# Low halves of the first weights and of V's weights on VectorE alone, and the last result's operands scaled ahead of their products

## The chip, the cores and the metric

The kernel runs on one core of one Trainium2 chip. The metric is the time of one execution on the device, in microseconds (us); smaller is better. The engines are named as in the profile: PE is TensorE's matmul, PEld its weight load, DVE is VectorE, ACT is ScalarE, POOL is GpSimd and SP is SyncE, whose queue issues most of the transfers.

## The reference, cut to what matters

For an input x of 2048 rows by 512 columns, attention with a sliding window of 256 (32 heads of 16) and a gated feed-forward layer are computed from the same x, and a gate per row mixes them:

```
x = A_x
g = sigmoid((x * gate_w).sum(-1, keepdims=True))
a = attention(x @ wqkv, window 256) @ wo
b = (silu(x @ w_gate) * (x @ w_up)) @ w_down
out = g * a + (1 - g) * b
```

## The kernel before

**Products.** Every fp32 operand of a product is split into a high half, rounded to the matmul's own fp32 format, and a low half, which is the rest. A product of two operands is three matmuls: high by high, high by low, low by high. The function `split` (L67 to L73) makes the halves: the high one is a copy (L70, here always on ACT), and the low one is the subtraction of L73, `lo = src - hi`, on the engine that the caller names. The instruction at L73 waits for the one at L70.

**Order.** The order of the instructions on each engine is the order in which the program text emits them (a manual schedule); each engine goes through its own list in that order and waits where an operand is not there. A tile name has a fixed number of buffers; a tile that takes over a buffer waits for the last use of the one before.

**Start.** SP's queue loads, in this order, pieces of the first two groups' query and key weights (`wqk`), the four parts of x's first 512 rows (`xT[0]`), the four parts of V's weights (`wv`) and the rest of x. `split_wq(g, n, lo_eng)` splits piece n of the weights of group g: piece 0 is the first 128 columns, piece 1 the other 384. `split_x(c, ks)` splits parts ks of x's chunk c. PE begins with `proj` of groups 0 and 1 on x's chunk 0 (24 matmuls into the tile `pa`, three for a group and part in turn), then `vproj(0)` to `vproj(3)`, V for four blocks of 128 rows (12 matmuls each into the tile `pb`, which has two buffers; `put_v` on ACT empties them, L443), then `proj` on chunks 1 to 3 (L232 for all of these). `fill_rows` sets memory on POOL, and POOL also makes the low halves of the projections' results (`split_qk`).

**Middle.** Attention's scores, weights and values for eight groups are woven with the feed-forward's first two products; PE has no gap there.

**End.** The feed-forward's last product is computed as a seven-product block scheme; `ITEMS` lists its steps in order, and `halve(e)` splits the operand of a step four steps ahead into `HALF[e]` (tiles `hh`, `hl`). The last stage of the scheme is stage 4, and the last three of its steps (from `end`) are drained by hand: the first of the two results, (2, 2), gets its three products with `block(e, (0,))`; then the last result, (2, 3), gets its three products in two halves of 256 columns, with an own PSUM tile `pa`. `GATE[1]` holds 1 - g, and `scaled` multiplies a result by it (L952), adds the part from attention (L954) and sends it (L956). For (2, 3) `rest` is that sum without the last three steps. The end before the change is:

```
scaled(2, 3, rest, two[1], send=False)
for e in ITEMS[end:]:
    block(e, (0,))
scaled(2, 2, t, two[0])
...
    nc.vector.tensor_tensor(out=part[:, cols], in0=ps, in1=GATE[1][:, 2, cols], op=ALU.mult)
    nc.vector.tensor_tensor(out=part[:, cols], in0=part[:, cols], in1=rest[:, cols], op=ALU.add)
    nc.sync.dma_start(place(2, 3)[:, cols], part[:, cols])
```

Of the kernel before, what the change touches and what calls it, by code (L numbers as in the profile page):

```python
# [9 lines left out]
F32 = mybir.dt.float32  # L10
F32R = mybir.dt.float32r
AF = mybir.ActivationFunctionType
ALU = mybir.AluOpType
# [3 lines left out]
P = 128  # L17
S, D, H, DH, W, F = 2048, 512, 32, 16, 256, 1792
NK = D // P
NB = S // P  # L20
CH = 512
# [15 lines left out]
def gated_mix(ctx, tc, xT, xn, wqk, wv, wo, wgu, wd, gw, outT):  # L37
# [4 lines left out]
    nc = tc.nc  # L42
# [18 lines left out]
    ring = ctx.enter_context(tc.tile_pool(name="ring", bufs=2))  # L61
# [6 lines left out]
    def split(hi, lo, src, hi_eng, lo_eng):  # L68
        if hi_eng is nc.scalar:
            nc.scalar.copy(hi, src)  # L70
        else:
            hi_eng.tensor_copy(hi, src)
        lo_eng.tensor_tensor(out=lo, in0=src, in1=hi.bitcast(F32), op=ALU.subtract)  # L73

    def fetch(src, raw=None):

        raw = ring.tile([P, D], F32, name="raw", bufs=1) if raw is None else raw
        nc.sync.dma_start(raw, src)
        return raw

    def by_k(t):
        return t.rearrange("p (k n) -> p k n", k=NK)
# [11 lines left out]
    def run(gen, n=None):  # L94

        while n is None or n > 0:
            if next(gen, run) is run:
                break
            n = n and n - 1
# [73 lines left out]
    def prefetch():  # L173
        if WKEYS:
            PEND.append(weights(WKEYS[0], lo_eng=nc.vector if WKEYS.pop(0) == ('f', NF - 1, 0) else nc.gpsimd))
# [25 lines left out]
    with ExitStack() as A:  # L201
# [14 lines left out]
        def kept():  # L216
            return sm.tile([P, CH], F32, name="ev", bufs=EV)
# [10 lines left out]
        def whole(pool, name, todo, done):  # L228

            ps = pool.tile([P, CH], F32, name=name)  # L230
            for n, (w, x) in enumerate(todo):
                nc.tensor.matmul(ps, w, x, start=n == 0, stop=n == len(todo) - 1)  # L232
                if n < len(todo) - 1:
                    yield
            done(ps)
            yield
# [166 lines left out]
        wvh = vpool.tile([P, NK, D], F32R, name="wvh")  # L403
        wvl = vpool.tile([P, NK, D], F32R, name="wvl")
# [8 lines left out]
        def split_wq(g, n, lo_eng):  # L413
            if n == 0:
                WT["p", g] = [ring.tile([P, D], F32R, name=w) for w in ("wh", "wl")]
            hi, lo = (w[:, QUARTERS[n]] for w in WT["p", g])
            split(hi, lo, WQ[g][:, QUARTERS[n]], nc.scalar, lo_eng)
            if n == 1:
                WT["p", g] = [by_k(w) for w in WT["p", g]]
# [3 lines left out]
        def fill_rows(tiles, value, hf, eng):  # L423
            for t in tiles:
                eng.memset(halves_of(t)[hf].bitcast(F32), value)
# [3 lines left out]
        def fill_v(t):  # L429
            nc.gpsimd.memset(t, 0.0)  # L430
            for i in range(2):
                nc.gpsimd.memset(t[:, :, i, :68].rearrange("p g (j e) -> p g j e", e=17)[:, :, :, DH], 1.0)
# [3 lines left out]
        def v_products(b):  # L436
            c, o = divmod(b * P, CH)
            return [(xt[c][:, k, o:o + P], wt[:, k]) for k in range(NK)
                    for xt, wt in ((xhi, wvh), (xhi, wvl), (xlo, wvh))]

        def put_v(b, ps):
            t = vs[b // 2 % 2]
            nc.scalar.copy(t[:, :, b % 2, :68].rearrange("p g (j e) -> p g j e", e=17)[:, :, :, :DH],  # L443
                           ps.rearrange("p (g j e) -> p g j e", j=4, e=DH))
            if b % 2:
                nc.gpsimd.dma_start(vd[:, :, b - 1:b + 1].rearrange("g p b e -> p g (b e)"),
                                    t.rearrange("p g b e -> p g (b e)"))

        def vproj(b):
            return whole(pp, "pb", v_products(b), lambda ps: put_v(b, ps))  # L450
# [11 lines left out]
        def split_x(c, ks=range(NK)):  # L462
            for k in ks:
                split(xhi[c][:, k], xlo[c][:, k], xraw[2 * c + k // 2][k % 2], nc.scalar, nc.vector)

        for c in range(NCH):
# [7 lines left out]
            if c == 0:  # L474
                wvraw = [fetch(wv[:, k], kept()) for k in range(NK)]
        split_wq(0, 0, nc.gpsimd)
        split_x(0, range(1))
        split_wq(1, 0, nc.vector)
        split_wq(0, 1, nc.gpsimd)
        fill_rows(KT[0], 1.0, 0, nc.gpsimd)  # L480
        split_x(0, range(1, 2))
        split_wq(1, 1, nc.vector)
        split_x(0, range(2, NK))
        for k in range(NK):
            split(wvh[:, k], wvl[:, k], wvraw[k], nc.scalar, nc.vector if k % 2 else nc.gpsimd)
        prefetch()
        both = [proj(g, 0, pp, "pa") for g in range(2)]
        for k in range(NK):
            for gen in both:
                run(gen, 3)  # L490
        split_x(1)
        fill_v(vs[1])
        fill_rows(QT[0], 0.0, 1, nc.gpsimd)
        fill_rows(KT[0], 1.0, 1, nc.gpsimd)
        for b in range(2):
            run(vproj(b))
        split_x(2)
        for b in range(2, 4):
            run(vproj(b))
# [198 lines left out]
        for t in range(G * NB + 1):  # L698
            g, i = divmod(t, NB)
            d, part = divmod(t, NSLOT)  # L700
# [31 lines left out]
    with ExitStack() as B:  # L732
        got = B.enter_context(tc.tile_pool(name="got", bufs=10, side="right"))
        hp = B.enter_context(tc.tile_pool(name="hp", bufs=LEAD + 2, side="right"))
# [5 lines left out]
        def column():  # L740
            return hp.tile([P, CH], F32, name="sg", bufs=4)

        def taken(src):
            t = got.tile([P, CH], F32, name="got")
            nc.sync.dma_start(t, src)
            return t

        def load_wo(k):
            raw = taken(wo[:, k])
            return lambda: split(woh[:, k], wol[:, k], raw, nc.scalar, nc.vector)  # L750
# [35 lines left out]
        ITEMS = [("a", c, k) for c in range(NCH) for k in range(NK)]  # L786
# [4 lines left out]
        SRC, HALF, PARTS = {}, {}, {}  # L791
# [34 lines left out]
        def spare(m):  # L826
            return PLACE[5][:, 2 + m] if m < 2 else PLACE[6][:, m]
# [65 lines left out]
        GATE = {}  # L893
# [71 lines left out]
        def after(p, pr):  # L965

            two = bank(p, pr)
            for d in range(2):
                m = 2 * pr + d
                if p == 1:  # L970
                    JOBS.append(lambda d=d, m=m: nc.scalar.copy(saved(m), two[d]))
                if p == 5:
                    JOBS.append(lambda d=d, m=m: nc.scalar.copy(saved(4 + m), two[d]))
                if p == 6:
                    JOBS.append(lambda d=d, m=m: nc.vector.tensor_tensor(out=spare(m), in0=two[d], in1=saved(4 + m), op=ALU.subtract))
                if p == 2:
                    JOBS.append(lambda d=d, m=m: combined(2 * pr, d, two[d], saved(m), ALU.add))
                if p == 7:
                    JOBS.append(lambda d=d, m=m: combined(2 * pr + 1, 2 + d, two[d], saved(4 + m), ALU.subtract))
                if p == 3:  # L980
                    JOBS.append(lambda d=d, m=m: combined(2 * pr + 1, d, two[d], spare(m), ALU.add))
                if p == 4 and pr == 0:
                    JOBS.append(lambda d=d: scaled(2 * pr, 2 + d, column(), two[d]))

        late = [load_wo(k) for k in range(NK)]
        for e in ITEMS[:LEAD]:
            load(e)
# [21 lines left out]
        end = len(ITEMS) - 3  # L1009

        DO = {}

        def on(n, f, *args):
            DO.setdefault(n, []).append(lambda: f(*args))

        for j in range(2 * NP):
            two = divmod(j, 2)
            n = WO + j
# [20 lines left out]
        for i in range(NP):  # L1039
            n = WO + 57 + 4 * (i // 2) + i % 2 - (i == 6)  # L1040
            steps(n, (n + 6, n + 7), negated, NP + i)
        for n, e in enumerate(ITEMS[:end]):
            if n + LEAD + AHEAD < WO:
                load(ITEMS[n + LEAD + AHEAD])
            for f in DO.pop(n, ()):
                f()
            while rows and at[(*rows[0], 0)] <= n + 6:
                load_sum(*rows.pop(0))
            if n + LEAD < len(ITEMS):
                halve(ITEMS[n + LEAD])  # L1050
            if JOBS:
                JOBS.pop(0)()
            if e[0] == "a":
                multiply_a(*e[1:])
                continue
            p, k, pr = e
            block(e)
            HALF.pop(e)
            if k == NP - 1:
                after(p, pr)  # L1060
        while JOBS:
            JOBS.pop(0)()
        two, t, part, rest = bank(4, 1), *(column() for _ in range(3))
# [4 lines left out]
        for cols in (slice(0, CH // 2), slice(CH // 2, CH)):  # L1068
            ps = pp.tile([P, CH], F32, name="pa")[:, cols]
            for n, (p, k, pr) in enumerate(ITEMS[end:]):  # L1070
                hh, hl = HALF[p, k, pr]
                mm3(ps, [(block_weights(p, k, 1), (hh[:, cols], hl[:, cols]))], start=n == 0, stop=n == 2)
            nc.vector.tensor_tensor(out=part[:, cols], in0=ps, in1=GATE[1][:, 2, cols], op=ALU.mult)
            nc.vector.tensor_tensor(out=part[:, cols], in0=part[:, cols], in1=rest[:, cols], op=ALU.add)
            nc.sync.dma_start(place(2, 3)[:, cols], part[:, cols])


# [32 lines left out]
```

## Time and profile before

| | before |
|---|---|
| median of 3 runs | 803.44 us (803.0 to 803.46) |
| the profiled execution's own time | 803.47 us |
| its span, first to last instruction | 801.8 us |
| PE busy | 795.2 us, 99% of the span |
| DVE busy | 627.3 us, 78% |
| ACT busy | 432.4 us, 54% |
| POOL busy | 346.2 us, 43% |
| granted TensorE clock | 1.0 of full speed |

The span is what the rows below show; 1.67 us of the profiled execution's time lie around it. A row of the timeline has the start, the duration, the engine, the line, the operation, the tiles written and read, the shapes and the count, and in brackets how long the engine stood idle before it and what ended that.

### The profile page before, as it was taken

To read this page: it belongs to the slowest core of one execution; us is meant where nothing else is said; L and a number is where in the kernel's file an instruction comes from. 1 tells how busy PE (TensorE), PEld (TensorE's weight loads), DVE (VectorE), ACT (ScalarE), POOL (GpSimd) and SP (SyncE) were. 2 spreads that over 40 slices of the span, in tenths; PEclk is the share of its full clock that TensorE was granted. 3 is DMA by queue.
4 is the path that set the end of the run, shared out by engine and by line. 5 is a ranking of instruction groups with operands and counts; after the bars stand their busy time and mean duration, and the time that the engine had idled before them with its cause. 6 is when DMAs were issued, how large, how long until landed. Compare 5 with 4: busy or idle time off the path is not lost.

```text
span 801.8 us, 21443 instructions
## 1 busy us (share of the span) xinstructions
PE 795.2 (99%) x8247; PEld 697.1 (87%) x8247; DVE 627.3 (78%) x1686; ACT 432.4 (54%) x883; POOL 346.2 (43%) x647
## 2 busy tenths in 40 slices
PE   8999999999999999999999999999999999999998
PEld 7888999989889989889998988888988888888886
DVE  6397687878887787878777878888675478899896
ACT  6412656666566566555666656555643235554642
POOL 7821546564546556544656454546740111000212
PEclk9999999999999999999999999999999999999999
DMA  8675414434252453351444516435627898718435
GB/s 298 171 200 164 141 57 135 119 114 137 71 164 78 117 167 94 113 163 54 134 119 130 152 46 200 134 99 181 195 100 240 283 342 300 290 56 275 93 54 104
DMA packets 62107, 121.88 MB, mean 152 GB/s; under 512 B 10868, under 2 KB 19828, under 8 KB 61748
## 3 DMA queue, kind: packets, MB, share of 16 engines
q1 hardware_dynamic: 54900, 99.27, 40.1%
q0 software_dynamic: 7104, 21.24, 9.0%
q8 instruction: 65, 1.06, 0.6%
q14 instruction: 38, 0.31, 0.1%
HBM read 55.97 MB, written 39.34 MB: 119 GB/s over the span
## 4 chain that ended last, share of the span: by engine, by line
PE 96%; DVE 2%; DMA 1%; SPq 0%; POOL 0%; issue 0%; ACT 0%
PE pa L252 24%; PE pb L252 24%; PE ps L302 7%; PE ps L344 5%; PE ps L368 5%; PE ps L89 4%; PE ps L90 4%; PE ps L88 4%; PE pb L368 4%; PE pb L232 2%; PE pb L89 2%; PE pa L89 2%; PE pa L90 2%; PE pb L90 2%; PE pa L88 2%; PE pb L88 2%
## 5 line engine op out<-in xcount | busy, mean ns | idle before, releaser
L304 DVE CUSTOM_DVE_ANT_0 ps<-ps,mask 128x384 f32<-128x384 f32 (+2 forms) x512 | 268.4, 540 | 99.4 <-PE ps L344 52.3
L346 ACT ACTIVATE pt<-ps 128x384 f32<-128x384 f32 (+2 forms) x512 | 238.0, 474 | 127.8 <-PE ps L344 68.0
L348 POOL TENSOR_SCALAR_AFFINE_SELECT pt<-pt 128x256 f32<-128x256 f32 x256 | 110.2, 431 | 198.6 <-ACT pt L346 196.8
L344 PE MATMUL ps<-q,k 64*128 64x384 f32 (+2 forms) x512 | 162.3, 334 | 0.0
L302 PE MATMUL ps<-k,q 63*128 63x384 f32 (+2 forms) x512 | 159.8, 332 | 0.5 <-DVE mx L304 0.5
L252 PE MATMUL pb<-xhi,wh 64*128 64x512 f32 x512 | 116.9, 395 | 0.0
L252 PE MATMUL pb<-xlo,wh 64*128 64x512 f32 x512 | 115.6, 391 | 0.0
L252 PE MATMUL pb<-xhi,wl 64*128 64x512 f32 x512 | 115.6, 391 | 0.0
L252 PE MATMUL pa<-xhi,wh 64*128 64x512 f32 x512 | 115.3, 393 | 0.0
L252 PE MATMUL pa<-xlo,wh 64*128 64x512 f32 x512 | 114.2, 391 | 0.0
L252 PE MATMUL pa<-xhi,wl 64*128 64x512 f32 x512 | 114.2, 391 | 0.0
L302 PEld LDWEIGHTS ps<-k,q 63*128 63x128 f32 x512 | 88.7, 185 | 14.1 <-DVE mx L304 3.7
L351 POOL TENSOR_SCALAR_AFFINE_SELECT pt<-pt 128x256 f32<-128x256 f32 x224 | 98.6, 440 | 0.0
L344 PEld LDWEIGHTS ps<-q,k 64*128 64x128 f32 x512 | 91.1, 184 | 4.9 <-ACT pt L346 0.2
L304 DVE DVE_READ_ACCUMULATOR2_ANT mx<- 128x1 f32 x512 | 71.3, 139 | 0.0
L368 PE MATMUL ps<-pt,vg 64*32 64x320 f32 (+4 forms) x1408 | 70.6, 344 | 0.0
L368 PE MATMUL pb<-pt,vg 64*32 64x256 f32 (+3 forms) x1360 | 69.9, 349 | 0.0
L252 PEld LDWEIGHTS pb<-xhi,wh 64*128 64x128 f32 x512 | 62.8, 185 | 4.1 <-DVE o L385 0.3
L252 PEld LDWEIGHTS pb<-xhi,wl 64*128 64x128 f32 x512 | 62.4, 184 | 3.5
L252 PEld LDWEIGHTS pa<-xhi,wl 64*128 64x128 f32 x512 | 61.1, 185 | 3.9
L252 PEld LDWEIGHTS pb<-xlo,wh 64*128 64x128 f32 x512 | 62.5, 185 | 0.2
L252 PEld LDWEIGHTS pa<-xhi,wh 64*128 64x128 f32 x512 | 60.5, 186 | 1.8
(305 smaller groups left out, 1604.5 us busy)
## 6 DMA issues: line engine op xcount, KB each, us to landing
kept_h<-ev SPq DMA_DIRECT2D x52, 256.0 KB
od<-o POOLq DMA_DIRECT2D x32, 256.0 KB, 3.7
raw<-wgu SPq DMA_DIRECT2D x28, 256.0 KB
q<-xhi SPq DMA_DIRECT2D x56, 128.0 KB
k<-xhi SPq DMA_DIRECT2D x56, 128.0 KB
outT<-sg POOLq DMA_DIRECT2D x28, 256.0 KB, 4.4
vd<-vs POOLq DMA_DIRECT2D x8, 672.0 KB, 4.8
vg<-vd SPq DMA_DIRECT2D x32, 168.0 KB
```

The lines of the kernel that those rows point to most:

```text
L88: nc.tensor.matmul(ps, lh, rh, start=start and i == 0, stop=False, skip_group_check=skip)
L89: nc.tensor.matmul(ps, lh, rl, start=False, stop=False, skip_group_check=skip)
L90: nc.tensor.matmul(ps, ll, rh, start=False, stop=stop and i == n - 1, skip_group_check=skip)
L232: nc.tensor.matmul(ps, w, x, start=n == 0, stop=n == len(todo) - 1)
L252: mm = nc.tensor.matmul(ps[me], w[r], x[r], start=not second and i == 0, stop=bool(second) and i == n - 1)
L302: nc.tensor.matmul(ps[:, :n], QT[g % 2][pr][r, q0:q0 + P], KT[g % 2][pr][r, k0:k0 + n], start=True, stop=True)
L304: mx = nc.vector.tensor_tensor_reduce(out=ps[:, :n], in0=ps[:, :n], in1=mask[:, 3 * P - n:], scale=1.0, scalar=NEG, op0=ALU.add, op1=ALU.m ...
L344: nc.tensor.matmul(ps[:, :n], KT[g % 2][pr][r, k0:k0 + P], QT[g % 2][pr][r, k0:k0 + n], start=True, stop=True)
L346: BEHIND.append(nc.scalar.activation(pt[:, j, :n], ps[:, :n], AF.Exp, scale=SCALE))
L348: nc.gpsimd.affine_select(out=pt[:, :, :P], in_=pt[:, :, :P], pattern=[[0, 2], [1, P]], compare_op=ALU.is_ge, fill=0.0, base=0, channel_mu ...
L351: nc.gpsimd.affine_select(out=pt[:, :, 2 * P:], in_=pt[:, :, 2 * P:], pattern=[[0, 2], [-1, P]], compare_op=ALU.is_ge, fill=0.0, base=-1, ...
L368: nc.tensor.matmul(AV[g, c][h][32 * j:32 * j + 32, q0 - c * CH:q1 - c * CH], VG[4 * g + kb // 4][o, kb % 4, 17 * j:17 * j + 32], PT[g, kb, ...
```

## The change

At the start, the low half of piece 1 of group 0's weights goes from POOL to DVE, and so do the low halves of parts 0 and 2 of V's weights (parts 1 and 3 were on DVE). The split of x's chunk 1 is moved from before `vproj(0)` to two parts behind `vproj(0)` and two behind `vproj(1)`; `fill_v` and the two `fill_rows` of POOL that stood behind it now stand ahead of the products. At the end, a new function `scaled_halves` multiplies the operand of each of the last three steps by the gate, into the single buffer of the tile `raw`, and splits the product; it is called three times in a row when the loop over the steps is over, ahead of `rest`. The last result's products then take these halves, and the multiplication by the gate behind the products is gone.

```diff
         split_wq(1, 0, nc.vector)
-        split_wq(0, 1, nc.gpsimd)
+        split_wq(0, 1, nc.vector)
...
-            split(wvh[:, k], wvl[:, k], wvraw[k], nc.scalar, nc.vector if k % 2 else nc.gpsimd)
+            split(wvh[:, k], wvl[:, k], wvraw[k], nc.scalar, nc.vector)
...
-        split_x(1)
         fill_v(vs[1])
         fill_rows(QT[0], 0.0, 1, nc.gpsimd)
         fill_rows(KT[0], 1.0, 1, nc.gpsimd)
         for b in range(2):
             run(vproj(b))
+            split_x(1, range(2 * b, 2 * b + 2))
...
+        SCALED = []
+
+        def scaled_halves(i):
+
+            e = ITEMS[end + i]
+            raw = ring.tile([P, D], F32, name="raw", bufs=1)
+            nc.vector.tensor_tensor(out=raw, in0=PARTS["v", e[1], e[2]], in1=GATE[1][:, 2], op=ALU.mult)
+            SCALED.append([ring.tile([P, D], F32R, name=w) for w in ("wh", "wl")] if i < 2 else
+                          [hp.tile([P, CH], F32R, name=w) for w in ("hh", "hl")])
+            split(*SCALED[i], raw, nc.scalar, nc.vector)
...
         DO = {}
+        DO[end] = [lambda i=i: scaled_halves(i) for i in range(3)]
...
+        for f in DO.pop(end):
+            f()
         while JOBS:
             JOBS.pop(0)()
...
-                hh, hl = HALF[p, k, pr]
+                hh, hl = SCALED[n]
                 mm3(ps, [(block_weights(p, k, 1), (hh[:, cols], hl[:, cols]))], start=n == 0, stop=n == 2)
-            nc.vector.tensor_tensor(out=part[:, cols], in0=ps, in1=GATE[1][:, 2, cols], op=ALU.mult)
-            nc.vector.tensor_tensor(out=part[:, cols], in0=part[:, cols], in1=rest[:, cols], op=ALU.add)
+            nc.vector.tensor_tensor(out=part[:, cols], in0=ps, in1=rest[:, cols], op=ALU.add)
             nc.sync.dma_start(place(2, 3)[:, cols], part[:, cols])
```

## Rows read from the trace of the kernel before

**Rows 1.** The page: PE's busy time, and the chain that ended last.

```profile
PE 795.2 (99%) x8247; PEld 697.1 (87%) x8247; DVE 627.3 (78%) x1686; ACT 432.4 (54%) x883; POOL 346.2 (43%) x647
...
PE 96%; DVE 2%; DMA 1%; SPq 0%; POOL 0%; issue 0%; ACT 0%
```

**Rows 2.** The chain in order of time, 0 to 45 us (start, us, what).

```profile
4.56 6.43 DMA ev<-wv
...
13.01 1.72 POOL wvl L73
...
24.36 10.88 PE pa L232 x48
```

**Rows 3.** Timeline 0 to 36 us, PE's matmuls around its waits.

```profile
8.43 0.50 PE L232 MATMUL pa<-xlo,wh 128*128 128x512 f32 x1
...
13.05 0.50 PE L232 MATMUL pb<-wvl,xhi 128*128 128x512 f32 x1 [0.43 <-POOL wvl L73]
...
13.39 0.40 PE L232 MATMUL pb<-wvh,xlo 128*128 128x512 f32 x1
...
16.03 0.39 PE L232 MATMUL pb<-wvh,xhi 128*128 128x512 f32 x1
```

**Rows 4.** Timeline 0 to 45 us, ACT, DVE and POOL at the start.

```profile
6.82 1.01 POOL L73 TENSOR_TENSOR wl<-raw,wh 128x384 fp32r<-128x384 f32 x1 [2.03 <-ACT wh L70]
...
7.29 1.08 DVE L73 TENSOR_TENSOR xlo<-q,xhi 128x512 fp32r<-128x512 f32 x1 [1.76 <-ACT xhi L70]
...
7.77 1.84 POOL L425 MEMSET k<- 128x1024 f32 x2
...
8.30 0.55 DVE L73 TENSOR_TENSOR wl<-ev,wh 128x384 fp32r<-128x384 f32 x1
...
8.77 0.68 DVE L73 TENSOR_TENSOR xlo<-q,xhi 128x512 fp32r<-128x512 f32 x1
...
11.02 2.57 ACT L70 CAST wvh<-ev 128x512 fp32r<-128x512 f32 x4 [0.96 <-DMA ev<-wv]
...
17.85 0.58 ACT L443 COPY vs<-pb 128x512 f32<-128x512 f32 x1
```

**Rows 5.** Groups by line, 10 to 15 us: V's low halves on either engine.

```profile
L73 POOL TENSOR_TENSOR wvl<-ev,wvh 128x512 fp32r<-128x512 f32 x2 | 3.0, 1495 | 2.1 <-ACT wvh L70 2.1
L73 DVE TENSOR_TENSOR wvl<-ev,wvh 128x512 fp32r<-128x512 f32 x2 | 2.9, 1436 | 1.6 <-ACT wvh L70 1.5
```

**Rows 6.** Timeline 770 to 803 us, DVE and ACT at the end.

```profile
789.52 0.62 ACT L70 CAST hh<-xlo 128x512 fp32r<-128x512 f32 x1 [0.73 <-DVE hl L73]
...
789.43 0.69 DVE L952 TENSOR_TENSOR sg<-ps,xlo 128x512 f32<-128x512 f32 x1
790.18 0.69 DVE L73 TENSOR_TENSOR hl<-xlo,hh 128x512 fp32r<-128x512 f32 x1
793.61 0.69 DVE L952 TENSOR_TENSOR sg<-ps,xlo 128x512 f32<-128x512 f32 x1 [2.73 <-PE ps L90]
794.33 0.69 DVE L954 TENSOR_TENSOR sg<-sg,k 128x512 f32<-128x512 f32 x1
...
796.37 0.69 DVE L954 TENSOR_TENSOR sg<-sg,k 128x512 f32<-128x512 f32 x1
796.98 0.42 DVE L1073 TENSOR_TENSOR sg<-pa,xlo 128x256 f32<-128x256 f32 x1
797.43 0.42 DVE L1074 TENSOR_TENSOR sg<-sg 128x256 f32<-128x256 f32 x1
797.79 0.42 DVE L1073 TENSOR_TENSOR sg<-pa,xlo 128x256 f32<-128x256 f32 x1
798.25 0.42 DVE L1074 TENSOR_TENSOR sg<-sg 128x256 f32<-128x256 f32 x1
```

**Rows 7.** Timeline 770 to 803 us, SP's queue: the last issues.

```profile
797.09 0.34 SPq L956 DMA_DIRECT2D outT<-sg  x1
797.88 1.15 SPq L1075 DMA_DIRECT2D outT<-sg  x2
```

**Rows 8.** Waits of SP's queue, 20 to 60 us (total, times, longest).

```profile
SPq L285 <- ACT xhi L70: 12.0, 1, 12.0
SPq L286 <- POOL x01lo L73: 2.3, 1, 2.3
```

**Rows 9.** Timeline 669.5 to 672 us, DVE: four subtractions that overwrite each other's inputs.

```profile
669.93 1.79 DVE L192 TENSOR_TENSOR xlo<-xlo 128x256 f32<-128x256 f32 x4
```

## The prediction

> **What bounds the kernel now.** I read the page first. PE is busy for 795.2 of the span's 801.8 us, and the chain that ended last is 96% PE [rows 1]. So a gain can only come where PE waits or where PE is over: at the start and at the end. The chain in order of time shows what is not PE at the start: the transfer of V's weights until 10.99, then POOL's low halves of them, and from there to the end of the projections PE alone [rows 2]. PE's own timeline gives the waits: a matmul at 8.43 behind x's low half, one at 13.05 behind POOL's `wvl` [rows 3]. The timelines of ACT, DVE and POOL show why those halves were late [rows 4, 5]. At the end I read DVE: it stands idle for 2.73 us until 793.61, works nearly without a stop from 795.64, and the last addition ends at 798.67 [rows 6]; the last transfer is issued 0.02 us later, and the span ends 3.11 us after that issue [rows 7].
>
> One measure of this kernel can tell some 0.2% from no change, 1.61 us.
>
> **The start, first weights.** POOL's low half of piece 1 took 1.01 us from 6.82, and x's low half on DVE beside it took 1.08 us from 7.29; the same subtraction with no such neighbour takes 0.68, and the 384 columns take 0.55 on DVE with the next one 0.47 behind it [rows 4]. On DVE the piece starts at 6.82 at the latest, is over at 7.37, x's low half starts at 7.29 as before and is over at 7.97 instead of 8.37. PE's matmul of 8.43 comes 0.40 earlier. The two memory sets of POOL that followed move ahead; one of them ran beside the 0.55 and the 0.68 [rows 4], so they slow nothing.
>
> **The start, V's weights.** The four high halves come every 0.64 us from 11.02 (2.57 over 4) [rows 4]. Low halves take 1.44 on DVE and 1.50 on POOL while both engines work on them [rows 5]; on DVE alone I take the 0.68 of [rows 4]. The four low halves are then over at 12.36, 13.0, 13.65 and 14.3 (high half, about 0.04 us, 0.68). PE, from 8.03, reaches V's first low half 17 matmuls of 0.227 (10.88 over 48 [rows 2]) later, at about 12.0, waits for it until 12.45, needs 0.34 to the next matmul as it does after such a wait (13.05 to 13.39 [rows 3]) and then 0.227 for each. So the other three low halves are wanted at 13.25, 13.93 and 14.61, each after it is there, and `vproj(1)` begins at 12.45 + 0.34 + 10 x 0.227 = 15.06 where it began at 16.03 [rows 3]: 0.97 us gained. Bounds: nothing, if the low halves still take 1.44, and 1.6, if PE never waited again after 8.03 (28 matmuls of 0.227 end at 14.39); the first wait for V stays, since its weights land at 10.99, so I take 0.97.
>
> **The start, what is moved.** x's chunk 1 is split later, but PE needs it only at 24.36 [rows 2], some 23.4 in the new order. ACT works in the order put_v(0), two copies of 0.62, put_v(1), two copies; put_v(0) was held back by the four copies until 17.85 [rows 4] and comes at about 15.8 now. That matters: `vproj(2)` takes put_v(0)'s PSUM buffer at 15.06 + 2.72 = 17.78, before the old copy would have been over (18.43). Unmoved, 0.65 of the gain would be lost. ACT has the last of the four copies done near 19.8 (`vproj(1)` ends at 17.78, then put_v(1) at 0.58 and two copies at 0.62), and DVE the last low half near 20.5, 3 us ahead of its use; those of chunk 2 follow about where they were. SP's queue for the stacked queries and keys waits on ACT's halves of the projections [rows 8], and these follow PE; POOL, which has less to do now, follows too. So the 0.97 us is carried through the middle, in which PE is never idle for long.
>
> **The end, what is added.** The three calls stand in DVE's list behind the low half of 790.18 and ahead of `rest` (793.61). Each is a product on DVE (0.69), a copy on ACT (0.62) and a subtraction on DVE (0.69), and each waits for the one before; the next call's product overwrites `raw`, which has one buffer. Nothing of one call overlaps the next. The step from DVE to ACT costs 0.70 from start to start and that from ACT to DVE 0.66 (789.52 to 790.18) [rows 6]. Between the subtraction and the product that overwrites its input I take 0.73: in [rows 9] four instructions of this kind take 1.79, so 0.46 from start to start where independent ones of that size follow after 0.36 (797.43 to 797.79 [rows 6]), and a dependent pair of 512 columns needs 0.72 (793.61 to 794.33 [rows 6]); the lower bound is 0.61, the step of independent ones (796.37 to 796.98). A call is thus 0.70 + 0.66 + 0.73 = 2.09.
>
> From 790.79 (790.18 + 0.61), in the old clock: products at 790.79, 792.88, 794.97; the last subtraction at 796.33, over at 797.02. Then `rest` from 796.94 (before: 793.61), its addition 797.66, (2, 2)'s product 798.27, its addition 798.99 to 799.68 (before: to 797.06), and the two additions of the last result at 799.60 and 799.96, over at 800.38. Two multiplications of 0.42 are gone, but 798.67 becomes 800.38, 1.71 us later: of the 6.2 us that the calls take, the idle 2.73 us cover less than half.
>
> PE is not what ends last: its third operand's low half comes at 797.02, and the ten or so matmuls of 256 columns that are left (half of 0.227 each) are over near 798.4, before DVE reaches the last addition. SP's queue has (2, 2) at 799.70 and the two halves right behind it, 0.34 each [rows 7] where 0.8 lay between them: the last is issued at 800.4 to 800.6, with 0.1 between two, against 798.69. I take 1.9 for the whole end: 1.71, 0.1 for the issues, 0.1 for three transfers (512 KB) that go one right behind the other. Bounds: a gain of 0.45 (797.79 to 798.25 is what the last multiplication takes), if all of the new work hid; a cost of 1.5 with the step of 0.61 and nothing from the queue; 2.3 if the transfers hold each other up for another 0.4.
>
> The Trainium skill's page "VectorE: DVE Perf Modes" ("The DRAIN you can't avoid") has it that the next operation starts only when the pipeline is empty; the same page allows an earlier start for an operation that isn't held. The rows here show 0.61 from start to start at a duration of 0.69. By the strict rule the four independent steps behind the last subtraction would add 0.3, and the sum would be 804.7; the row decides.
>
> **Sum.** 803.47 - 0.97 + 1.9 = 804.4 for an execution like the profiled one; the median of the runs shown is 0.03 lower, so 804.4 stands: 0.12% slower, which is within 0.2%.
>
> **The rivals.** *The gain of the start is not kept (slower, 0.17).* Place: the 16 to 45 us, where ACT, POOL and SP's queue pace the stacked operands of the first scores; POOL's 2.3 us in SP's wait [rows 8] speak for it. Against it: these queues themselves start from PE's projections. With none of it kept the time is 805.4; beyond 805.05 it is slower by over 0.2%, so it decides once less than 0.3 us is kept. *The end is hidden (0.12).* If DVE's three calls ran before 793.61, only the last multiplication would be gone: 803.47 - 0.97 - 0.45 = 802.05, faster by 0.18%; it needs a chain of 2.8 us where the rows give 6.2, or the calls further ahead in DVE's list. *The change of engine gains nothing (part of the 0.17).* If DVE's subtractions of V's weights were slowed by the transfers that fill memory then and not by POOL, they would stay at 1.44, one after another, and PE would wait longer than before. Against it: 0.68 at 8.77, with transfers running.
>
> **How the numbers follow.** The forecast has 0.65, with a range of its own of 804.0 to 804.8; the rivals have 0.17 and 0.12, and 0.06 is left for a shift in the middle of either sign. The range of 803.0 to 805.5 holds the forecast, the slow rival and a part of the last; what is left out is the hidden end and half of the last, 0.15 to 0.2. Faster by over 0.2% needs more than 1.61 us, so the hidden end and a further gain: 0.05. Slower by over 0.2%: 0.17 for the rival, of which some stays below 805.05, and the upper bound of the end: 0.17 in all. Same: 0.78.
>
> **What the profile would show.** Right: `wvl` four times on DVE at some 0.68 to 0.7; `vproj(1)` at about 15.06; the first scores some 1 us earlier; at the end three products on DVE 2.09 apart, DVE's idle 2.73 us split into waits for ACT, and the last addition over near 799.4, with the start's gain taken off. Wrong: if V's low halves stay above 1 us; if PE shows a new wait between 16 and 45 us; if the calls stand less than 1.9 apart; or if the last transfer's way to the end of the span differs from 3.1 us.

## The result, and the profile after

The changed kernel takes 804.69 us (median of 22 runs, 804.02 to 805.8) where the kernel before takes 803.52 (22 runs, 802.54 to 804.38): a ratio of 1.0015, interval 1.0009 to 1.0021. That is 0.7 to 1.7 us slower: the interval lies wholly above a ratio of 1, but at 0.15% the difference is inside the 0.2% that the prediction counts as no change. The profiled execution's span is 802.9 us where it was 801.8.

**The start.** The chain in order of time of the kernel after (start, us, what), to be held against [rows 2]:

```profile
2.66 4.18 DMA raw<-wqk
...
6.86 0.51 ACT wh L70
7.37 0.53 ACT xhi L70
7.90 0.04 issue
7.94 4.65 PE pa L232 x18
12.59 10.88 PE pb L232 x48
23.47 10.88 PE pa L232 x48
```

V's weights have left the chain: from 7.94 on it is PE alone. What stands ahead of PE now is the transfer of piece 1 of group 0's weights. PE comes to `proj(0,1)` (group 0 on x's chunk 1) at 23.47 where it came at 24.36 [rows 2], 0.89 us earlier. PE's timeline of the kernel after has its matmul with x's low half, the first with V's low half and the first of `vproj(1)`:

```profile
8.67 0.50 PE L232 MATMUL pa<-xlo,wh 128*128 128x512 f32 x1
...
12.66 0.39 PE L232 MATMUL pb<-wvl,xhi 128*128 128x512 f32 x1
...
15.15 0.39 PE L232 MATMUL pb<-wvh,xhi 128*128 128x512 f32 x1
```

The timeline and the groups by line of the kernel after show DVE's part:

```profile
7.40 0.56 DVE L73 TENSOR_TENSOR wl<-raw,wh 128x384 fp32r<-128x384 f32 x1 [1.87 <-ACT wh L70]
7.92 0.69 DVE L73 TENSOR_TENSOR xlo<-q,xhi 128x512 fp32r<-128x512 f32 x1
...
11.56 2.65 DVE L73 TENSOR_TENSOR wvl<-ev,wvh 128x512 fp32r<-128x512 f32 x4 [1.03 <-ACT wvh L70]
```

```profile
L73 DVE TENSOR_TENSOR wvl<-ev,wvh 128x512 fp32r<-128x512 f32 x4 | 2.6, 693 | 1.0 <-ACT wvh L70 1.0
```

x's low half takes 0.69 instead of 1.08 [rows 4], and each of V's four 0.69 instead of 1.44 on DVE or 1.50 on POOL [rows 5]: DVE does four in less time (2.65) than the two took before (2.9). It does so beside the same transfers: the DMA engines' busy share from 8 to 16 us is 0.99, and it was 1.00 before. So the prediction's rival that the transfers, and not POOL, had slowed these subtractions falls. And the put_v(0) of the changed order, on ACT, comes at 15.67 and not at 17.85 [rows 4]:

```profile
15.67 0.58 ACT L443 COPY vs<-pb 128x512 f32<-128x512 f32 x1
```

**The end.** DVE's timeline of the kernel after, to be held against [rows 6]; L991 is the product by the gate, L1087 the one addition that is left:

```profile
789.13 0.69 DVE L73 TENSOR_TENSOR hl<-xlo,hh 128x512 fp32r<-128x512 f32 x1
789.74 0.69 DVE L991 TENSOR_TENSOR raw<-got,xlo 128x512 f32<-128x512 f32 x1
791.12 0.69 DVE L73 TENSOR_TENSOR wl<-raw,wh 128x512 fp32r<-128x512 f32 x1 [0.69 <-ACT wh L70]
791.84 0.69 DVE L991 TENSOR_TENSOR raw<-xlo,xlo 128x512 f32<-128x512 f32 x1
793.26 0.69 DVE L73 TENSOR_TENSOR wl<-raw,wh 128x512 fp32r<-128x512 f32 x1 [0.73 <-ACT wh L70]
793.99 0.69 DVE L991 TENSOR_TENSOR raw<-xlo,xlo 128x512 f32<-128x512 f32 x1
795.45 0.69 DVE L73 TENSOR_TENSOR hl<-raw,hh 128x512 fp32r<-128x512 f32 x1 [0.76 <-ACT hh L70]
796.06 0.68 DVE L952 TENSOR_TENSOR sg<-ps,xlo 128x512 f32<-128x512 f32 x1
...
798.10 0.69 DVE L954 TENSOR_TENSOR sg<-sg,k 128x512 f32<-128x512 f32 x1
798.71 0.75 DVE L1087 TENSOR_TENSOR sg<-pa,sg 128x256 f32<-128x256 f32 x2
```

The last low half of the loop starts 1.05 us earlier than before (789.13 against 790.18), so the start's gain came through the middle. From there it is lost. DVE, idle for 2.73 us in one stretch before, is now idle three times (0.69, 0.73 and 0.76 us), each time for ACT's copy, and `rest` starts 6.93 us behind that low half where it started 3.43 behind it. The span ends 802.9 - 789.13 = 13.77 us behind it, where it ended 801.8 - 790.18 = 11.62 behind it: the end costs 2.15 us. 2.15 - 1.05 = 1.1 is the difference of the spans. (Spans are printed to 0.1 us, so sums with them are good to some 0.1; by the executions' own times, 803.47 and 804.63, the end costs 2.2.)

The last transfers: SP's queue, and the stretches in which the transfers moved data (the last two columns are the busy share of the DMA engines and GB/s), of the kernel after:

```profile
798.82 0.34 SPq L956 DMA_DIRECT2D outT<-sg  x1
799.26 0.88 SPq L1088 DMA_DIRECT2D outT<-sg  x2
```

```profile
799.00:800.00 1.00, 0.00 (x0) 0.00 (x0) 0.46 (x2) 0.00 (x0) 0.00 (x0) 1.00 0.32 125
800.00:801.00 1.00, 0.00 (x0) 0.00 (x0) 0.00 (x0) 0.00 (x0) 0.00 (x0) 0.66 1.06 382
```

Before, SP issued the three transfers at 797.09, 797.88 and 798.70 [rows 7], some 0.8 us apart. Now the issues come 0.44 apart, at 798.82, 799.26 and 799.70, the last of them 0.24 behind the end of the last addition (799.46) where it was 0.03 behind it, and the transfers fill the DMA engines one right behind the other for a whole microsecond.

### The profile page after: what moved, and what is told of

The parts are those of the page before. It is cut to its first block, busy times and chain, and to the rows that moved or that the text cites. A ratio compares the mean times of both kernels' runs of the same rounds, so it can differ in the third digit from the quotient of the medians.

```text
span 802.9 us, 21454 instructions
## 1 busy us (share of the span) xinstructions
PE 794.1 (99%) x8247; PEld 696.3 (87%) x8247; DVE 629.4 (78%) x1693; ACT 434.2 (54%) x886; POOL 341.5 (43%) x644
## 3 DMA queue, kind: packets, MB, share of 16 engines
q8 instruction: 65, 1.06, 0.6%
## 4 chain that ended last, share of the span: by engine, by line
PE 92%; DVE 5%; ACT 1%; issue 1%; DMA 1%; SPq 0%; DVEq 0%; ACTq 0%
PE pa L252 24%; PE pb L252 24%; PE ps L302 6%; PE ps L344 5%; PE ps L368 5%; PE pb L368 4%; PE ps L90 3%; PE ps L88 3%; PE ps L89 3%; PE pb L232 2%; PE pa L232 2%; DVE hl L73 1%; PE pa L777 1%; PE pb L777 1%; PE pb L90 1%; PE pa L90 1%
```

## The experiments

The kernel before was run again beside the others, in three groups; its medians there were 803.55, 803.72 and 803.65 us. Intervals are some 0.0009 to either side, 0.7 us, which is as much as most of the differences below. So a ratio seldom decides by itself, and the spans and places in the traces, one execution of each kernel, are read beside the ratios. "Behind the loop" is the time from the start of the loop's last low half on DVE to the end of the span: 11.62 before, 13.77 after.

**The start alone** (the end as before):

```diff
-        split_wq(0, 1, nc.gpsimd)
+        split_wq(0, 1, nc.vector)
...
-            split(wvh[:, k], wvl[:, k], wvraw[k], nc.scalar, nc.vector if k % 2 else nc.gpsimd)
+            split(wvh[:, k], wvl[:, k], wvraw[k], nc.scalar, nc.vector)
...
-        split_x(1)
...
             run(vproj(b))
+            split_x(1, range(2 * b, 2 * b + 2))
```

> The start of the change alone; the end as before. Theory (the change is a gain of 1.0 at the start and a cost of 2.1 at the end): 1.0 us faster than before, ratio 0.9988, V's four low halves at about 0.66 each and everything behind them about 1 us earlier, down to the last transfer. Rival (the start's gain is eaten in the middle, the end costs only 1.1): no change, ratio 1.000.

Measured: 802.53 us, ratio 0.9988 (0.9979 to 0.9997), 1.0 us faster. Behind the loop 801.0 - 789.45 = 11.55, as before. In its profile PE comes to `proj(0,1)` at 23.63 and the loop's last low half starts at 789.45, both 0.73 earlier than before. The gain of the start is real and kept; the rival falls. How large it is, 0.7 in the profile or 1.0 by the medians, is within the interval of 0.2 to 1.7 us.

**The end alone** (the start as before; the diff is the end's part of the change):

> The end of the change alone; the start as before. Theory: 2.1 us slower than before, ratio 1.0026, the three products on DVE 2.1 us apart and the last transfer issued 10.6 to 10.7 us behind the start of the last low half of the loop. Rival (the start's gain is eaten, the end costs only 1.1): 1.1 us slower, ratio 1.0014.

Measured: 806.0 us, ratio 1.0028 (1.0018 to 1.0039), 2.4 us slower. Behind the loop 804.2 - 790.43 = 13.77, as in the whole change. The three products stand 2.10 and 2.14 apart there, and the last transfer is issued at 800.98, 10.55 behind that low half. Start and end add up within what the intervals allow: -1.0 and +2.4 by the medians, or -1.05 and +2.15 in the profile after, against the +1.1 to +1.2 of the whole.

**The start without the move** of the split of x's chunk 1 (the diff is against the start alone):

```diff
+        split_x(1)
         fill_v(vs[1])
...
             run(vproj(b))
-            split_x(1, range(2 * b, 2 * b + 2))
```

> The start's two changes of engine without the move of the split of x's chunk 1; the end as before. Theory (the four copies on ACT hold back put_v(0), and vproj(2) waits for its PSUM buffer): 0.5 us of the gain is lost, 0.5 us faster than before, ratio 0.9994, and PE shows a wait of about 0.5 us near 18 us. Rival (the move is worth nothing): 1.0 us faster, as the start alone, with no wait of PE there.

Measured: 803.31 us, ratio 0.9996 (0.9987 to 1.0005). PE's timeline of this kernel:

```profile
17.34 0.39 PE L232 MATMUL pb<-wvh,xlo 128*128 128x512 f32 x1
18.25 0.50 PE L232 MATMUL pb<-wvh,xhi 128*128 128x512 f32 x1 [0.52 <-ACT vs L443]
18.59 0.39 PE L232 MATMUL pb<-wvl,xhi 128*128 128x512 f32 x1
```

PE waits for put_v(0) with the first matmul of `vproj(2)`: 0.91 to that matmul and 0.34 to the next, where 0.227 each is the pace, so 0.8 us are lost. By the medians it is 802.53 against 803.31, the same 0.8, though their intervals overlap. The rival, which expected no such wait, falls: the move keeps most of the start's gain.

**The products first.** The whole change, but the three products by the gate stand together, each written over its own operand, and the splits behind them:

```diff
+        def scale_part(i):
+            raw = PARTS[("v", *ITEMS[end + i][1:])]
+            nc.vector.tensor_tensor(out=raw, in0=raw, in1=GATE[1][:, 2], op=ALU.mult)
+
         def scaled_halves(i):
-            e = ITEMS[end + i]
-            raw = ring.tile([P, D], F32, name="raw", bufs=1)
-            nc.vector.tensor_tensor(out=raw, in0=PARTS["v", e[1], e[2]], in1=GATE[1][:, 2], op=ALU.mult)
+            raw = PARTS[("v", *ITEMS[end + i][1:])]
...
-        DO[end] = [lambda i=i: scaled_halves(i) for i in range(3)]
+        DO[end] = [lambda i=i, f=f: f(i) for f in (scale_part, scaled_halves) for i in range(3)]
```

> The whole change, but at the end the three products by the gate stand together in DVE's list, each written over its own operand, and the three splits behind them. Theory (the end's cost is the chain product, copy, subtraction, next product): the copies on ACT now run beside DVE, the six DVE operations are over about 4.4 us behind the start of the last low half of the loop where they took 7.0, the last addition waits for PE again, the end gains 0.45 and with the start the kernel is 1.5 us faster than before, ratio 0.9981. Rival (the end's cost is the added work itself, six operations of 0.61 in DVE's list against 2.73 idle, or the transfers that come close together): 0 to 0.5 us slower than the start alone, ratio about 0.999 to 1.000.

Measured: 802.06 us, ratio 0.9982 (0.9974 to 0.9991), 1.5 us faster than before, and so faster than the kernel before and the kernel after. DVE and then ACT in the timeline of this kernel:

```profile
789.63 0.69 DVE L73 TENSOR_TENSOR hl<-xlo,hh 128x512 fp32r<-128x512 f32 x1
790.24 0.68 DVE L990 TENSOR_TENSOR got<-got,xlo 128x512 f32<-128x512 f32 x1
790.84 1.29 DVE L990 TENSOR_TENSOR xlo<-xlo,xlo 128x512 f32<-128x512 f32 x2
792.05 0.69 DVE L73 TENSOR_TENSOR wl<-got,wh 128x512 fp32r<-128x512 f32 x1
792.65 0.68 DVE L73 TENSOR_TENSOR wl<-xlo,wh 128x512 fp32r<-128x512 f32 x1
793.25 0.68 DVE L73 TENSOR_TENSOR hl<-xlo,hh 128x512 fp32r<-128x512 f32 x1
...
797.25 0.42 DVE L1090 TENSOR_TENSOR sg<-pa,sg 128x256 f32<-128x256 f32 x1 [0.33 <-PE pa L90]
```

```profile
790.96 0.62 ACT L70 CAST wh<-got 128x512 fp32r<-128x512 f32 x1 [1.36 <-DVE got L990]
791.61 0.63 ACT L70 CAST wh<-xlo 128x512 fp32r<-128x512 f32 x1
792.24 0.62 ACT L70 CAST hh<-xlo 128x512 fp32r<-128x512 f32 x1
```

The same nine instructions: DVE's six now follow one another in 0.60 to 0.61, without a wait, and ACT's three run beside them. They are over 4.3 us behind the loop's last low half, and the last addition waits for PE. Behind the loop: 800.8 - 789.63 = 11.17, 0.45 less than before, which is the multiplication that is gone (0.46 in [rows 6]). Its last issue comes 0.03 behind the last addition (797.70 against 797.67), although the three issues are 0.44 and 0.65 apart. So it was neither the added work nor three transfers in a row by themselves that made the end slower.

**The order kept, each product in its own place.** Here the single buffer is taken away and the order of the calls is not:

```diff
-            raw = ring.tile([P, D], F32, name="raw", bufs=1)
-            nc.vector.tensor_tensor(out=raw, in0=PARTS["v", e[1], e[2]], in1=GATE[1][:, 2], op=ALU.mult)
+            raw = PARTS["v", e[1], e[2]]
+            nc.vector.tensor_tensor(out=raw, in0=raw, in1=GATE[1][:, 2], op=ALU.mult)
```

> The whole change, with each product by the gate written over its own operand instead of into the single buffer of raw; the order of the calls stays product, copy, subtraction, next product. Theory (the order in DVE's list makes the chain: the subtraction waits for ACT, and the next product stands behind it): only the step from the subtraction to the next product falls from 0.72 to 0.61, so the end is 0.2 us shorter, 0.9 to 1.0 us slower than before, ratio 1.0012. Rival (the single buffer makes the chain): the calls overlap, the end gains as with the products first, ratio about 0.998.

Measured: 804.57 us, ratio 1.0012 (1.0003 to 1.0021). DVE's timeline of this kernel:

```profile
789.82 0.69 DVE L991 TENSOR_TENSOR got<-got,xlo 128x512 f32<-128x512 f32 x1
791.19 0.69 DVE L73 TENSOR_TENSOR wl<-got,wh 128x512 fp32r<-128x512 f32 x1 [0.69 <-ACT wh L70]
791.80 0.68 DVE L991 TENSOR_TENSOR xlo<-xlo,xlo 128x512 f32<-128x512 f32 x1
793.22 0.69 DVE L73 TENSOR_TENSOR wl<-xlo,wh 128x512 fp32r<-128x512 f32 x1 [0.73 <-ACT wh L70]
793.83 0.69 DVE L991 TENSOR_TENSOR xlo<-xlo,xlo 128x512 f32<-128x512 f32 x1
```

Only the step from a subtraction to the next product falls, 0.72 to 0.61. Behind the loop 802.8 - 789.21 = 13.59, 0.2 less than the whole change. By this trace the single buffer costs 0.2 us and the order costs the rest; the medians of the two kernels (804.57 and 804.69) are too near to tell. The rival, that the buffer makes the chain, falls.

**Only piece 1's low half on DVE** (V's on both engines, the split moved):

```diff
-        split_wq(0, 1, nc.gpsimd)
+        split_wq(0, 1, nc.vector)
```

> Of the start only the low half of piece 1 of group 0's weights on DVE, with the moved split; V's low halves and the end as before. Theory (PE comes earlier to V's weights and waits there for POOL's low half of them, which follows their landing): no gain, 0 to 0.2 us, ratio 0.9998 to 1.000. Rival (the waits add up): 0.4 us faster, ratio 0.9995.

**Only V's low halves on DVE** (piece 1's on POOL, the split moved):

```diff
-            split(wvh[:, k], wvl[:, k], wvraw[k], nc.scalar, nc.vector if k % 2 else nc.gpsimd)
+            split(wvh[:, k], wvl[:, k], wvraw[k], nc.scalar, nc.vector)
```

> Of the start only V's four low halves on DVE, with the moved split; piece 1's low half stays on POOL and the end as before. Theory (V's low halves alone are what held PE, and 0.4 us of the gain need PE to be there earlier): 0.6 to 0.8 us faster, ratio 0.9991. Rival (all of the gain is V's): 1.0 us faster, ratio 0.9988.

Measured: 803.11 us, ratio 0.9993 (0.9984 to 1.0002), for piece 1 alone; 802.49 us, ratio 0.9985 (0.9976 to 0.9994), for V alone. V's part gives as much as both together (0.9988), which the theory put lower; the interval of piece 1's part has a ratio of 1 in it. The medians (0.6 and 1.2 us faster) don't divide the gain of 1.0, but the traces do. Their chains, piece 1 alone and then V alone (start, us, what):

```profile
10.56 0.63 ACT wvh L70
...
23.90 10.88 PE pa L232 x48
```

```profile
11.25 0.63 ACT wvh L70
...
23.60 10.88 PE pa L232 x48
```

V's weights land at another time in each execution, so PE's place at `proj(0,1)` is counted from the start of ACT's first copy of them. It is 24.36 - 11.02 = 13.34 us in the kernel before [rows 2, 4], 23.90 - 10.56 = 13.34 with piece 1 alone and 23.60 - 11.25 = 12.35 with V alone. So in these traces piece 1 alone gains nothing: PE waits for POOL's halves of V's weights as before, and the 0.46 us that its profile is ahead (24.36 - 23.90) is the 0.46 by which those weights came earlier. This is the theory's account and speaks against the rival, though the median lies on the rival's side. V alone gains 0.99 where PE waits for V's weights, nearly the 0.97 of the prediction and more than the theory's 0.6 to 0.8. Piece 1's part counts where V's weights are there first, as in the profile after: they alone would have let PE come at 10.91 + 12.35 = 23.26 (an estimate from these two profiles), and it came at 23.47, held by the first weights.

**Result (2, 2) sent on ACT's queue:**

```diff
-                    nc.sync.dma_start(place(c, d), t)
+                    nc.scalar.dma_start(place(c, d), t)
```

> The whole change, with result (2, 2) sent on ACT's queue instead of SP's. Theory (three issues right behind each other on one queue hold back the last by 0.34 us behind its addition): the last issue comes 0.3 us earlier and the kernel is 0.8 to 0.9 us slower than before, ratio 1.0011. Rival (the transfers, not the issues, set the end of the span): no difference to the whole change, 1.1 us slower, ratio 1.0015.

Measured: 804.67 us, ratio 1.0013 (1.0004 to 1.0022): no difference to the whole change. Its timeline has SP's two issues at

```profile
799.18 0.84 SPq L1088 DMA_DIRECT2D outT<-sg  x2
```

and behind the loop it takes 803.0 - 789.16 = 13.84. The last issue came only 0.1 us earlier (799.57 against 799.70), so the run says less than it should; but what it gained did not shorten the span. The busy share of the DMA engines says why: 0.27, 1.05 and 0.13 in the three microseconds from 799, and 0.32, 1.06 and 0.06 in the kernel after. The transfers move one behind another in both, so that an earlier issue only waits longer. This speaks for the transfers and against the issues.

**Piece 1 loaded ahead of part 1 of x**, with the products first:

```diff
                 if c == k == 0:
                     fetch_wq(1, 0)
+                    fetch_wq(0, 1)
                 if c == 0 and k == 1:
-                    fetch_wq(0, 1)
                     fetch_wq(1, 1)
```

> The products first at the end, and at the start piece 1 of group 0's weights loaded ahead of part 1 of x instead of behind it. Theory (the landing of that piece, then two copies on ACT, sets when PE goes on near 7.4 us): its copy on ACT starts near 5.8 instead of 6.0 to 7.0, PE goes on 0.3 us earlier, 1.8 us faster than before, ratio 0.9978. Rival (part 1 of x now lands as late as the piece did, or PE's wait behind it at V's weights takes the gain back): as with the products first, 1.5 us faster, ratio 0.9982.

Measured: 802.0 us, ratio 0.998 (0.9971 to 0.9988): not to be told from the products first (802.06), and between the ratios that theory and rival expected, so the trace has to decide. ACT's timeline of this kernel:

```profile
6.01 0.51 ACT L70 CAST wh<-raw 128x384 fp32r<-128x384 f32 x1 [1.21 <-DMA raw<-wqk]
6.92 0.62 ACT L70 CAST xhi<-q 128x512 fp32r<-128x512 f32 x1 [0.39 <-DMA q<-xT]
```

The piece is there earlier, but now ACT waits for part 1 of x, and PE goes on at 7.59 where it went on at 7.42 with the products first. The theory falls; the rival holds.

**The products first, piece 1's low half on POOL** (in `split_wq(0, 1, ...)`, `nc.vector` back to `nc.gpsimd`):

> The products first at the end, V's low halves on DVE, but the low half of piece 1 of group 0's weights back on POOL. Theory (that part of the change gains only where V's weights don't hold PE anyway): within 0.4 us of the products first, 1.2 to 1.5 us faster than before, ratio 0.9983. Rival (the 0.4 us at 8.43 are kept in full): 1.1 us faster, ratio 0.9986.

Measured: 802.33 us, ratio 0.9983 (0.9974 to 0.9992), 0.3 us from the products first, less than these runs can tell. Its trace shows the step itself: x's low half takes 1.08 us beside POOL again, and PE's matmul with it comes at 8.86, 2.20 behind the start of ACT's copy of piece 1 (6.66), where it comes 1.82 behind it with the products first (8.15 and 6.33). What of these 0.4 us reaches the end it doesn't tell: part 3 of x landed late in this execution (ACT's copy of it at 10.55, and at 9.19 in the profile after) and held PE once more.

## Why the prediction was right, point by point

**The start's gain: right in its sizes, in part by luck in its place.** 0.97 was forecast; 1.0 was measured alone, with an interval of 0.2 to 1.7. V's low halves take 0.69 on DVE alone, and `vproj(1)` begins at 15.15 where 15.06 was forecast. But the step "the first wait for V stays" did not hold in the profile after. Piece 1 landed later there: ACT's copy of it starts at 6.86, and in the kernel before at

```profile
6.22 0.51 ACT L70 CAST wh<-raw 128x384 fp32r<-128x384 f32 x1 [1.49 <-DMA raw<-wqk]
```

So PE reached V's first low half at 12.66 and not at about 12.0. The half was ready at 12.25, and the wait went instead of being shortened. That a later arrival without a wait comes out within 0.1 us of an earlier one with a wait is luck. With V alone, where PE does wait for V's weights, the forecast's own step is measured, 0.99.

The 0.40 of the first weights is hidden in the profile after by the late landing, but not gone: from the start of ACT's copy of piece 1 to PE's matmul with x's low half it took 2.21 us before (6.22 to 8.43 [rows 3]) and 1.81 after (6.86 to 8.67). The other three kernels with that half on POOL have 2.19 to 2.20, and the other six with it on DVE and the same order of loads have 1.81 to 1.82.

The Trainium skill's page "SBUF — State Buffer" ("Who interferes with whom") says that a VectorE instruction with two SBUF inputs contends with a GpSimd instruction that reads SBUF and not with one that only writes it. This case agrees: 1.44 beside POOL's subtractions [rows 5], 0.69 with POOL idle, and 0.68 beside POOL's memory set [rows 4].

**The move: right.** 0.65 us was forecast as the loss without it, 0.8 was measured, in the trace and by the medians.

**The middle carries it: right, though not to the tenth in every execution.** PE was 0.89 us ahead at 23.47 and the loop's last low half 1.05 at 789.13; the rival that the gain is not kept falls with the start alone, 0.73 at both places. In the profile of the products first, however, 1.31 us at 23.05 became 0.55 at 789.63, and PE waited 0.3 us for ACT between 550 and 575 us, which no other profile shows. That execution took 802.49 where the median is 802.06. (Nor is PE quite without a gap in the middle: in every profile it waits twice for DVE there, 0.5 us in all.)

**The end: the mechanism right, the size 0.25 to 0.3 short.** Forecast 1.9, measured 2.15 to 2.2. The products stand 2.10 and 2.15 apart (2.09 forecast): the step from subtraction to product took 0.72 and 0.73 (0.73 forecast) and that from ACT to DVE 0.65 to 0.66 (0.66), but that from DVE to ACT grew from 0.72 to 0.81 where 0.70 was taken. The 0.70 is the step of the loop before the change, from this row to ACT's copy at 789.52 [rows 6]:

```profile
788.82 0.69 DVE L73 TENSOR_TENSOR hl<-xlo,hh 128x512 fp32r<-128x512 f32 x1
```

ACT's copies in the kernel after stand 0.72, 0.77 and 0.81 behind the starts of the products (789.74, 791.84, 793.99):

```profile
790.46 0.62 ACT L70 CAST wh<-raw 128x512 fp32r<-128x512 f32 x1 [1.36 <-DVE raw L991]
792.61 0.62 ACT L70 CAST wh<-raw 128x512 fp32r<-128x512 f32 x1 [1.53 <-DVE raw L991]
794.80 0.62 ACT L70 CAST hh<-raw 128x512 fp32r<-128x512 f32 x1 [1.56 <-DVE raw L991]
```

The last addition ends 10.33 behind the start of the loop's last low half, where it ended 8.49 behind it: 1.84 later, 1.71 forecast. The rest, 0.31, lies behind the last addition (802.9 - 799.46 = 3.44 against 801.8 - 798.67 = 3.13), where 0.2 had been set down, 0.1 each for issues and transfers. Some 0.2 of it is the issues, since the last one is now 0.24 behind its addition; the way from the last issue to the end of the span is 802.9 - 799.70 = 3.2 against 3.1, about the 0.1 of the transfers. So the term for the issues was too small, and by the prediction's own numbers: (2, 2) at 799.70 and two issues 0.44 apart put the last at 800.58, 0.2 behind the 800.38 of its addition.

The prediction also gives 804.7 for the rule that each step takes the whole duration. That this is what was measured is chance: the independent steps took 0.60 to 0.61 again (795.45 to 796.06, 798.10 to 798.71), and the missing 0.3 lies in the places just named.

**The rival "the end is hidden"** was named with its condition, a chain of 2.8 us or a place further ahead. That condition was too strict. The products first meet the need in a third way: their six operations take 4.3 us, which delays `rest` but not the last addition, for which DVE waits on PE again. Then the end gains its 0.45.

For an execution like the profiled one 804.4 was forecast, and the profiled one took 804.63. The end cost 0.25 to 0.3 more than forecast, and the start gave 0.08 more (1.05 against 0.97).

## What to carry to other kernels

An engine's idle time covers added work only as far as that work can run without a wait. Three calls that go from one engine to another and back, each emitted whole, take three round trips, since the first engine's list stands still at every return. Emit all the first halves, then all the second: the same nine instructions went from a cost of 2.15 us to a gain of 0.45, of which the single buffer accounts for 0.2 and the order for the rest. And two engines that read the same memory may be no faster than one: VectorE alone finished all four subtractions sooner than the two engines that shared them. TensorE kept most of that gain only because the copies on ScalarE were reordered too, so that its next PSUM buffer came free in time.

## What was not expected of the hardware

The same transfers land at different times from one execution to the next, by more than parts of this change are worth: ACT's copy of piece 1 started at 6.03 to 7.00 us over the profiles with that order of loads, and its copy of V's first weights at 10.54 to 11.25. The step of a result from DVE to ACT took 0.72, 0.77 and 0.81 us in one row of three like instructions; the end alone shows the same three values (791.04 to 791.76, 793.14 to 793.91, 795.28 to 796.09), so it is not chance. With each product in its own place the step grows as well, 0.72, 0.76 and 0.79 (789.82 to 790.54, 791.80 to 792.56, 793.83 to 794.62). What it comes from stays open.

The 1.50 us of POOL's subtractions in [rows 5] is the mean of two unlike ones: the first took 1.29, as long as POOL takes with DVE idle (1.29 at 14.70 in the profile after), and the second, begun while DVE worked, 1.70. DVE's two took 1.23 and 1.64 where 0.69 is the time alone.
